# Moving one exponential behind a MoE evacuation in three units of an attention and MoE kernel

## The chip, the cores and the metric

The kernel runs on one core of one Trainium2 chip. The metric is the device time of one execution in microseconds (us). The time before is the median of three runs, 418.59 us (417.38 to 419.21). The profile is that of one further execution, which took 418.34 us.

The core's engines are called as in the profile: PE (TensorE, with PEld for its weight loads), ACT (ScalarE), DVE (VectorE), POOL (GpSimd) and SP (SyncE, which issues most DMAs). Each engine works through its own queue in order and waits on semaphores for the others.

## The reference

Attention with normalized queries and keys (8 batches, 12 heads, 448 positions, head size 64), followed by a two-layer MLP ("MoE") on 3584 tokens (768 to 2048 to 768):

```python
q_n, k_n = (rmsnorm(q, g_q), rmsnorm(k, g_k))
scores = scale * np.matmul(q_n, k_n.transpose(0, 1, 3, 2))
scores = scores - np.max(scores, axis=-1, keepdims=True)
attn = np.exp(scores)
attn = attn / (np.sum(attn, axis=-1, keepdims=True) + 1e-09)
x = np.matmul(attn, v)          # then heads side by side: (3584, 768)
h = x @ w_in
g = np.maximum(0.01 * h, h)
out = g @ w_out
```

## The kernel before

**Units and stages.** The attention is cut into 24 units, each one batch and four of its heads (three units make a batch). A unit has seven score tiles (t = 0 to 6), each of two PSUM banks. For u from 3 to 23 a unit runs through four stages, d = 0 to 3. In units 7 to 21 the scores (`score`, matmuls of line 222) of tile 0 are made in d = 0, of tiles 1, 2, 3 in d = 1, of 4, 5, 6 in d = 3 (`TRIPLES`). ACT turns each tile into exponentials (`ex`, line 242, tile `et`). `ex(u, 2)` issues the first two of a group of three straight behind the scores; the third is left in `st[u]["sT"]` and is issued later, in the unit's job list.

**MoE work between the stages.** The MLP of a batch already finished is kept in a list, `queue`, of small items. `fill(u, d, jobs)` takes as many items from it as the string `PLAN` says for this unit and stage (three in unit 8, d = 1; two in units 14 and 20, d = 1), and after each item it issues one entry of `jobs`: the remaining attention work of the stage. An item of the first layer (`moe1`) is six matmuls (line 420) into one PSUM bank and the evacuation of that bank by ACT with the leaky ReLU (`prelu`, line 414, into `gt`). Work that an item leaves for later (`later`) is issued when the next item begins (`flush`).

**The second layer** is done, for pairs of token tiles, with seven block products in place of eight (`seven`, items i0 to i6, matmuls of line 516), which need four sums of `gt` blocks made by DVE in the tile `sa`: s1 (line 497), s2 (line 500, which reads what s1 wrote), s3 (line 503) and s4 (line 506). For the first pair of an odd batch each sum is made in two halves of 128x512. i0 multiplies `gt` itself; i1 needs s2, i3 s1, i4 s3 and i5 s4. The second halves of s1 and s2 follow the last `moe1` item, whose evacuation they read; those of s3 and s4 follow i0.

**Where this meets.** In units 8, 14 and 20, d = 1, the two items taken first are the last two `moe1` items of batches 1, 3 and 5; behind them comes i0 and then i1. The jobs of that stage are the scaling of a transposed tile (`prep_g`, line 176), and the sums of squares (`prep_ssq`, line 180) with the sum of the first three exponential tiles (`add_e`, line 320, tiles 0 to 2). POOL's part in the stage is `xmul_pool` (line 376), the multiplication of the previous unit's output with the reciprocal softmax sums `rz`, which SP spreads by four DMAs (line 366). Further on in DVE's queue stand the copy of the first product (line 538), additions of products (line 523), the norms of unit u+2 (`prep_norm`, line 192, which need `rinv`, lines 185 and 186 on ACT; a transposing DMA, line 209, follows them) and, in the next unit, the row maximum (line 262) and its diagonal matrix `dg` (line 264), which PE takes in line 274.

PSUM has eight banks, given out by a list in the order in which they were dropped (`aux` for one, `slot` for a pair), so the order in which ACT's evacuations are written also decides which bank comes next. The order on every engine is the order of the Python text; no scheduler changes it.

Of the kernel before, what the change touches and what calls it, by code (L numbers as in the profile page):

```python
# [18 lines left out]
def kernel(  # L19
# [62 lines left out]
    def drop(tile_):  # L82
        for i in range(8):
            if tile_ is single[i]:
                assert i not in free
                free.append(i)
                return
        x = [i for i in range(4) if tile_ is double[i]][0]
        assert 2 * x not in free and 2 * x + 1 not in free
        free.extend((2 * x, 2 * x + 1))  # L90
# [134 lines left out]
    def qk(u, steps):  # L225
        st[u]["sT"] = []
        for t in steps:
            sT = slot()
            score(u, t, (sT[:, 0], sT[:, 1]))
            st[u]["sT"].append((t, sT))  # L230

    def ex(u, most=NS):
        s = st[u]
        if "et" not in s:
            s["et"] = epool.tile([P, NS, 2, S], FP16, tag="et", name="et")
        for t, sT in s["sT"][:most]:
            if isinstance(sT, list):
                for a in range(2):
                    nc.scalar.activation(s["et"][:, t, a], sT[a][:, 0:S], AF.Exp, bias=s["eb"], scale=1.0)
                    drop(sT[a])  # L240
            else:
                nc.scalar.activation(s["et"][:, t], sT[:, :, 0:S], AF.Exp, bias=s["eb"], scale=1.0)  # L242
                drop(sT)
        s["sT"] = s["sT"][most:]
# [6 lines left out]
    def shift_max(u):  # L251
        s = st[u]
        sT = s["sT"][0][1]
        if isinstance(sT, list):
            pm2 = small.tile([P, 2], FP32, tag="pm2", name="pm2")
            for a in range(2):
                nc.vector.tensor_reduce(pm2[:, a:a + 1], sT[a][:, 0:S], axis=AXL.X, op=ALU.max)
            s["spare"] = sT[0]
            nc.vector.tensor_reduce(s["spare"][:, 511:512], pm2, axis=AXL.X, op=ALU.max)
        else:  # L260
            s["spare"] = sT[:, 0]
            nc.vector.tensor_reduce(s["spare"][:, 511:512], sT[:, :, 0:S], axis=AXL.XY, op=ALU.max)  # L262
        s["dg"] = small.tile([P, P], FP16, tag="dg", name="dg")
        nc.vector.tensor_tensor(s["dg"], ident16, s["spare"][:, 511:512].broadcast_to([P, P]), op=ALU.mult)
# [22 lines left out]
    def gate(u):  # L287
        nc.gpsimd.tensor_copy(gate_t, buf(u, "n16")[:, 1, NS - 1, 1, D - 1:D])
# [38 lines left out]
    def zcol(u):  # L327
        s = st[u]
        s["zc"] = aux()
        ets = z_tiles(u)  # L330
        for i, e in enumerate(ets):
            for y in range(2):
                for a in range(2):
                    c = 32 * (2 * y + a)
                    nc.tensor.matmul(s["zc"][c:c + 32, 0:HS], onesr, e[:, a, HS * y:HS * y + HS],  # L335
                                     start=(i == 0), stop=(i == len(ets) - 1))

    def pv_slot(u):
        s = st[u]
        s["pslot"] = slot()  # L340
        s["pv"] = [s["pslot"][:, r] for r in range(2)]
        pv(u)
# [25 lines left out]
    def xmul_sb(u):  # L368
        xmul_pool(u, nc.vector)
# [76 lines left out]
    def flush(keep=0):  # L446
        kept = [p for p in pend if keep and (p[0] in (s1, s2, s3, s4) or hasattr(p[0], "waits") or keep == 5 and hasattr(p[0], "copies"))]
        now = [p for p in pend if p not in kept]
        pend[:] = kept
        for fn, args in now:  # L450
            fn(*args)
# [270 lines left out]
    def also(fn, *more):  # L722
        def both():
            fn()
            for m in more:
                m()
        return both
# [52 lines left out]
    def tripled(u):  # L780
        return 7 <= u < NU - 2

    def narrow(u):
        return 3 <= u < NU - 1
# [34 lines left out]
    with tc.manual_schedule():  # L819
# [203 lines left out]
        for u in range(3, NU):  # L1023
            for d in range(4):
                if u == 7 and d == 0:
                    shared.append(u)
                if d > 0 or u > 3:
                    qk(u, (TRIPLES if tripled(u) else STEPS)[d])
                    if d == 0:
                        shift_max(u)  # L1030
                        flush()
                        if u in (5, 6):
                            xmul_sb(u - 2)
                        if narrow(u - 1):
                            pv_slot(u - 1)
                            zcol(u - 1)
                            shift_mm(u)
                            pv_out(u - 1)
                        else:
                            zsum_slot(u - 1)  # L1040
                            pv(u - 1)
                            shift_mm(u)
                            zinv(u - 1)
                    ex(u, 2)
                    if d == 0 and narrow(u - 1):
                        zcol_ln(u - 1)
                if d == 2 and (u == 3 or ADDED.get(u, 0) > 3) and u < NU - 1:
                    add_e(u)
                    if u > 4:
                        xmul_sb(u - 1)  # L1050
                jobs = []

                def job(fn, *args):
                    jobs.append(lambda: fn(*args))

                if d == 0:
                    if u == 3:
                        prep_norm(4)
                        gate(4)
                    elif narrow(u - 1):  # L1060
                        if u < NU - 1:
                            job(zcol_inv, u - 1)
                    else:
                        xmul(u - 1)
                    if u + 4 < NU:
                        job(load, u + 4)
                    if u + 3 < NU:
                        load_v(u + 3)
                    if u < 6:
                        prep_sqp(u + 3)  # L1070
                if d == 1 and narrow(u - 1) and not 5 <= u < 8 and ADDED.get(u, 0) < 4:
                    xmul_pool(u - 1)
                if u == NU - 1:
                    if d == 1:
                        job(zcol_inv, u - 1)
                if fed(u, d) and u > 3:
                    push(u // NQ - 1)
                if (u, d) in ((3, 1), (4, 0)):
                    for ti in range(2):
                        prep_tr(u + 1, ti, VV)  # L1080
                if d == 1 and 5 <= u < NU - 1:
                    job(prep_g, u + 1)
                if u + 2 < NU:
                    if d == 1:
                        if ADDED.get(u) == 3 and u > 3:
                            job(lambda u: (prep_ssq(u + 2), add_e(u)), u)
                        else:
                            for ti in range(2):
                                job(prep_ssq, u + 2, ALL, (ti,))
                    if d == 2:  # L1090
                        job(prep_rinv, u + 2)
                        if u == 6:
                            job(xmul_sb, u - 1)
                        for ti in range(2):
                            job(prep_norm, u + 2, ALL, (ti,))
                        if u > 3:
                            job(prep_trd, u + 2)
                if d == 1 and 4 <= u < 8:
                    job(weight_sum, u - 4, 0)
                if d == 0 and 5 <= u < 9:  # L1100
                    job(weight_sum, u - 5, 1)
                if d == 1 and u == NU - 2:
                    jobs.append(lambda: None)
                    job(add_e, u)
                if u == NU - 2 and d == 0:
                    for n, tile_ in ((1, (raws, "rq", 3)), (2, (raws, "rk", 3)), (3, None), (4, (prep_p, "sq", 3))):
                        job(win_sum, n, 1, tile_)
                    for n in (3, 1, 2, 4):
                        job(x_sum, LATE, n)
                if u == NU - 1 and d == 3:  # L1110
                    job(add_e, u)
                    job(xmul_sb, u - 1)
                if d == 3 and 6 <= u < NU - 3:
                    for ti in range(2):
                        job(prep_sq, u + 3, ALL, (ti,))
                if st[u]["sT"]:
                    jobs[0:1] = [also(lambda: ex(u), *jobs[0:1])]
                fill(u, d, jobs)
        zsum_slot(NU - 1)
        pv(NU - 1)  # L1120
# [37 lines left out]
```

## Time and profile before

| | us |
|---|---|
| median of the runs (lowest to highest) | 418.59 (417.38 to 419.21) |
| the profiled execution | 418.34 |
| its span, first to last instruction | 416.6 |
| PE busy | 396.9 (95%) |
| DVE busy | 310.3 (74%) |
| ACT busy | 299.2 (72%) |
| POOL busy | 68.9 (17%) |
| mean granted clock of TensorE | 0.999 |

Busy time is what an engine's instructions cover; matmuls overlap each other, so a busy PE may still lose time between two starts. A timeline line gives the start in the span, the duration, engine, source line, operation, tile written and tiles read, shapes and count; in brackets, the idle time of that engine just before it and what ended it. A line of the list of waits gives who waited for whom, the total, the number of times and the longest.

### The profile page before, as it was taken

Reading aid. Unit: us, or ns where it says so; the run is one execution under the profiler, and the core shown is the slowest. Engines: PE = TensorE matmul, PEld = TensorE weight load, DVE = VectorE, ACT = ScalarE, POOL = GpSimd, SP = SyncE. Lnnn points to the kernel's source line nnn. Section 1 sums busy time; section 2 is a strip of 40 time slices with the busy share of each in tenths; the row PEclk is TensorE's granted clock in tenths of the full one; section 3 lists DMA queues with packets and bytes.
Section 4 is the critical chain, followed back from the end, with each engine's and each line's share of the span. In section 5 each row is a group of like instructions: output and inputs, shape, how many; then the busy total and the mean of one; then the engine's idle time right before and its main releaser. Section 6 shows DMA issues by size and latency. Waiting matters only on the chain.

```text
span 416.6 us, 9411 instructions
## 1 busy us (share of the span) xinstructions
PE 396.9 (95%) x3840; PEld 223.6 (54%) x3840; DVE 310.3 (74%) x490; ACT 299.2 (72%) x470; POOL 68.9 (17%) x70
## 2 busy tenths in 40 slices
PE   8688999999989999999989999999998999999996
PEld 7455454455445554555445554555454557558963
DVE  5997789899777766767668767678568888667772
ACT  5998977677958689878976689877994668653600
POOL 1887432200010100020020100003011201000000
PEclk9999999999999999999999999999999999999999
DMA  5999999898654895677663796577642451032014
GB/s 189 271 238 251 237 232 238 211 190 199 139 149 71 228 216 119 162 193 167 155 155 60 207 200 153 138 159 176 198 89 46 120 135 32 2 83 76 2 30 123
DMA packets 72526, 62.87 MB, mean 151 GB/s; under 512 B 36388, under 2 KB 67620, under 8 KB 72484
## 3 DMA queue, kind: packets, MB, share of 16 engines
q1 hardware_dynamic: 61888, 50.08, 46.8%
q0 software_dynamic: 10272, 11.80, 17.9%
q8 instruction: 30, 0.49, 0.5%
q10 hardware_dynamic: 324, 0.39, 0.3%
q14 instruction: 12, 0.10, 0.1%
HBM read 45.61 MB, written 11.01 MB: 136 GB/s over the span
## 4 chain that ended last, share of the span: by engine, by line
PE 72%; ACT 10%; DVE 10%; DMA 5%; issue 2%; SPq 0%; DVEq 0%; ACTq 0%
PE banks L516 22%; PE banks L420 22%; PE banks L222 7%; PE banks L648 6%; ACT et L242 6%; PE banks L398 5%; PE banks L466 4%; DMA qkT<-n 3%; PE banks L335 2%; ACT gt L414 2%; DVE n L192 2%; DVE sa L497 2%; DVE ssq L180 1%; DMA rk<-in_k_dram 1%; DMA out_dram<-ost 1%
## 5 line engine op out<-in xcount | busy, mean ns | idle before, releaser
L242 ACT ACTIVATE et<-banks,eb 128x896 f16<-128x896 f32 x166 | 160.3, 1015 | 29.3 <-PE banks L222 16.6
L420 PE MATMUL banks<-xt,win 128*128 128x448 f16 x612 | 122.2, 353 | 0.0
L420 PEld LDWEIGHTS <-win 128*128 128x128 f16 x612 | 57.3, 98 | 55.8 <-issue 6.5
L414 ACT ACTIVATE gt<-banks 128x448 f16<-128x448 f32 x104 | 56.7, 565 | 5.8 <-PE banks L420 4.6
L222 PE MATMUL banks<-qkT 64*64 64x448 f16 x672 | 50.8, 362 | 4.3 <-ACT et L242 3.4
L516 PE MATMUL banks<-tw,sa 128*128 128x384 f16 x264 | 47.4, 326 | 6.1 <-DVE sa L500 6.1
L180 DVE TENSOR_REDUCE ssq<-sq 128x14 f32<-128x896 f32 (+2 forms) x49 | 50.2, 1058 | 1.2 <-ACT sq L169 1.2
L516 PEld LDWEIGHTS <-sa 128*128 128x128 f16 x352 | 33.1, 98 | 31.5 <-DVE sa L500 7.3
L149 POOL DMA_DIRECT2D vt<-in_v_dram x24 | 17.9, 746 | 169.8 <-PE banks L398 169.5
L523 DVE TENSOR_TENSOR ost<-banks,ost 128x384 f32<-128x384 f32 x55 | 30.4, 553 | 17.2 <-PE banks L516 16.0
L398 PE MATMUL banks<-et,vt 64*64 64x448 f16 x672 | 37.0, 349 | 0.1
L222 PEld LDWEIGHTS <-qkT 64*64 64x64 f16 x672 | 17.9, 104 | 35.4 <-issue 28.4
L516 PEld LDWEIGHTS <-gt 128*128 128x128 f16 x264 | 25.5, 98 | 18.0 <-issue 1.4
L262 DVE TENSOR_REDUCE banks<-banks 128x1 f32<-128x896 f32 x22 | 24.1, 1096 | 14.7 <-PE banks L222 10.9
L466 PE MATMUL banks<-wout,gt 128*128 128x384 f16 x192 | 34.1, 327 | 0.0
L376 POOL TENSOR_TENSOR xt<-x,rz 128x896 f16<-128x896 f32 x9 | 19.4, 2159 | 81.8 <-DMA rz<-zs 74.3
L516 PE MATMUL banks<-wout,gt 128*128 128x384 f16 x176 | 32.4, 326 | 0.0
L192 DVE TENSOR_TENSOR n<-rq,rinv 128x896 f16<-128x896 f32 (+2 forms) x25 | 27.3, 1095 | 2.9 <-ACT rinv L186 2.9
L350 ACT COPY x<-banks 128x896 f32<-128x896 f32 x16 | 14.5, 906 | 20.6 <-DVE banks L275 20.6
L192 DVE TENSOR_TENSOR n<-rk,rinv 128x896 f16<-128x896 f32 (+2 forms) x26 | 27.5, 1065 | 0.0
L549 ACT COPY ost<-banks 128x384 f32<-128x384 f32 x11 | 5.3, 478 | 29.8 <-PE banks L516 29.7
L398 PEld LDWEIGHTS <-vt 64*64 64x64 f16 x672 | 20.3, 107 | 10.6 <-issue 0.4
(103 smaller groups left out, 482.9 us busy)
## 6 DMA issues: line engine op xcount, KB each, us to landing
rq<-in_q_dram SPq DMA_DIRECT2D x24, 448.0 KB, 4.3
rk<-in_k_dram SPq DMA_DIRECT2D x24, 448.0 KB, 4.7
out_dram<-ost SPq DMA_DIRECT2D x52, 192.0 KB, 3.5
rz<-zs SPq DMA_DIRECT2D x80, 112.0 KB, 2.3
vt<-in_v_dram POOLq DMA_DIRECT2D x24, 224.0 KB, 5.5
win<-in_moe_w_in_dram POOLq DMA_DIRECT2D x8, 384.0 KB, 15.8
wout<-in_moe_w_out_dram POOLq DMA_DIRECT2D x2, 1536.0 KB, 28.2
out_dram<-ost SPq DMA_DIRECT2D x4, 96.0 KB, 2.1
```

The lines of the kernel that those rows point to most:

```text
L180: nc.vector.tensor_reduce(buf(u, "ssq")[:, ti, :, c[0]:c[1]], buf(u, f"sq{ti}")[:, :, c[0]:c[1]], axis=AXL.X, op=ALU.add)
L192: nc.vector.tensor_tensor(buf(u, "n16")[:, ti, c[0]:c[1]].rearrange("p s a d -> p a s d"), src[:, :, c[0]:c[1]], buf(u, "rinv")[:, ti, :, ...
L222: nc.tensor.matmul(banks[a][64 * r:64 * r + 64, 0:S].rearrange("p (t x) -> p t x", t=NS), kT(u, r, a, t), qT(u, r, a), start=True, stop=True)
L242: nc.scalar.activation(s["et"][:, t], sT[:, :, 0:S], AF.Exp, bias=s["eb"], scale=1.0)
L262: nc.vector.tensor_reduce(s["spare"][:, 511:512], sT[:, :, 0:S], axis=AXL.XY, op=ALU.max)
L398: nc.tensor.matmul(s["pv"][r][64 * a:64 * a + 64, 0:S], vts[u % NV][64 * r:64 * r + 64, a, t], s["et"][64 * r:64 * r + 64, t, a], start=(t ...
L414: nc.scalar.activation(dst, src, AF.Prelu, bias=0.0, scale=1.0, alpha=0.01)
L420: nc.tensor.matmul(hps[:, 0:S], win16[:, kt // 2, kt % 2, ts(ft, P)], xt[:, kt // 2, kt % 2], start=(kt == 0), stop=(kt == KT - 1))
L466: nc.tensor.matmul(op2[:, 0:HC], gt[:, ft, ds(col(t), P)], wout16[:, ft, ds(HC * half, HC)], start=(i == 0), stop=(i == FT - 1))
L516: nc.tensor.matmul(bank[:, 0:HC], a[:, f], b[:, f], start=(first and f == 0), stop=(f == HF - 1), skip_group_check=not first)
L523: nc.vector.tensor_tensor(dst, g[name][:, 0:HC], src, op=ALU.add)
L648: nc.tensor.matmul(bank[:, HX * i:HX * i + HX].rearrange("p (t x) -> p t x", t=NS), w, x[:, kt], start=start, stop=(kt == HK - 1), skip_gr ...
```

## The change

```diff
                 if st[u]["sT"]:
-                    jobs[0:1] = [also(lambda: ex(u), *jobs[0:1])]
+                    n = 1 if d == 1 and u % 6 == 2 else 0
+                    jobs[n:n + 1] = [also(lambda: ex(u), *jobs[n:n + 1])]
                 fill(u, d, jobs)
```

The remaining exponential of a group is put in front of the first job, that is, behind the first MoE item. In units 8, 14 and 20 (u % 6 == 2, d = 1) it is now put in front of the second job, behind the second item. On ACT the order "evacuation, exponential of tile 3, evacuation" becomes "evacuation, evacuation, exponential of tile 3". The order on PE, DVE, POOL and SP stays as it was. Because the exponential's two banks are dropped after the second evacuation's bank, the PSUM pairs 4/5 and 6/7 take each other's place in what follows, from each of the three units on.

## The prediction

> **What bounds the kernel now.** I read the page's busy shares first, then the list of who waited for whom on TensorE, then the timeline around the longest wait, engine by engine. The page says that PE is the engine to follow:
>
> ```profile
> PE 396.9 (95%) x3840; PEld 223.6 (54%) x3840; DVE 310.3 (74%) x490; ACT 299.2 (72%) x470; POOL 68.9 (17%) x70
> ```
>
> The waits of PE (columns: total us, times, longest us) name one wait that is larger than all others:
>
> ```profile
> PE banks L516 <- DVE sa L500: 6.1, 3, 2.1
> PE banks L222 <- ACT et L242: 3.4, 8, 0.7
> ```
>
> Line 500 is s2, one of the four sums that feed the seven products. Its three waits lie at 123.0, 218.8 and 314.5 us, in units 8, 14 and 20: the units that the change touches. From 97 us to the end PE has no other gap over 0.08 us, so what is gained here has nothing else to hide behind. Unit 14 in the timeline (start, duration, engine, line; in brackets the idle time and what ended it):
>
> ```profile
> 214.01 0.60 ACT L414 ACTIVATE gt<-banks 128x448 f16<-128x448 f32 x1
> ...
> 214.44 1.07 ACT L242 ACTIVATE et<-banks,eb 128x896 f16<-128x896 f32 x1
> 214.60 1.46 PE L516 MATMUL banks<-wout,gt 128*128 128x384 f16 x8
> ...
> 215.32 0.62 ACT L414 ACTIVATE gt<-banks 128x448 f16<-128x448 f32 x1
> ...
> 215.89 2.06 POOL L376 TENSOR_TENSOR xt<-x,rz 128x896 f16<-128x896 f32 x1 [7.25 <-DMA rz<-zs]
> 215.90 0.81 PE L516 MATMUL banks<-tw,sa 128*128 128x384 f16 x4
> 215.97 2.26 DVE L497 TENSOR_TENSOR sa<-gt 128x512 f16<-128x512 f16 x1 [1.14 <-ACT gt L414]
> ...
> 218.27 0.42 DVE L500 TENSOR_TENSOR sa<-sa,gt 128x512 f16<-128x512 f16 x1
> 218.61 0.55 DVE L538 COPY ost<-banks 128x384 f32<-128x384 f32 x1
> 218.75 0.44 PEld L516 LDWEIGHTS <-sa 128*128 128x128 f16 x4 [2.43 <-DVE sa L500]
> 218.75 0.82 PE L516 MATMUL banks<-tw,sa 128*128 128x384 f16 x4 [2.04 <-DVE sa L500]
> 219.08 0.41 DVE L503 TENSOR_TENSOR sa<-gt 128x512 f16<-128x512 f16 x1
> ```
>
> The chain is: third exponential (214.44), second evacuation (215.32 to 215.94), s1 on line 497 (215.97), s2 (218.27), PE (218.75). What is long in it is s1: 2.26 us. Eleven microseconds earlier the other half of the same sums, the same shape, took this:
>
> ```profile
> 203.72 0.42 DVE L497 TENSOR_TENSOR sa<-gt 128x512 f16<-128x512 f16 x1
> 204.17 0.42 DVE L500 TENSOR_TENSOR sa<-sa,gt 128x512 f16<-128x512 f16 x1
> ```
>
> The difference is the multiplication on POOL (line 376), which starts 0.08 us ahead of s1 and ends at 217.95; s1 ends 0.28 later. So DVE stood still for POOL's whole instruction. That it works the other way round too, a third place shows:
>
> ```profile
> 280.98 1.09 DVE L192 TENSOR_TENSOR n<-rq,rinv 128x896 f16<-128x896 f32 x1
> 281.15 2.86 POOL L376 TENSOR_TENSOR xt<-x,rz 128x896 f16<-128x896 f32 x1 [7.93 <-DMA rz<-zs]
> ...
> 282.45 2.51 DVE L192 TENSOR_TENSOR n<-rk,rinv 128x896 f16<-128x896 f32 x1
> ```
>
> Here DVE began 0.17 us before POOL and kept its 1.09 us; POOL took 2.86 instead of its usual 2.06; and the next norm, begun inside POOL's time, took 2.51 instead of 1.08. Whoever starts first runs through. DVE instructions that read PSUM (the 0.55 us copies and additions) run at their usual length beside POOL.
>
> **The change, part by part.** Per unit one exponential (1.07 us shown, 0.90 from start to start) changes places with one evacuation on ACT. Nothing is added or removed; PE, DVE, POOL and SP keep their order, and no DMA is issued by the moved step or passed by it.
>
> *The evacuation comes earlier.* Now it starts at 215.32 because the exponential holds ACT. Without it, ACT is free at 214.44, but the matmuls of the second item must be done: their group ends at 214.76 by the PE timeline. Where an evacuation waits for such a group (ten times on this page), it starts 0.04 us after that end and takes 0.54: one at 100.71 follows a group that ends at 100.67. So it runs from 214.80 to 215.34 instead of ending at 215.94: 0.60 us earlier. ACT now waits 0.19 us for PE, a new wait. Behind it stand the exponential, then lines 185 and 186 (rinv).
>
> *s1 and s2.* s1 starts 0.03 us after the evacuation ends, as now: 215.37. DVE is free then (last addition of line 320 ended at 214.84). s1 takes 0.42 and ends at 215.79, and s2 starts 0.035 us behind it (0.03 to 0.04 in all pairs of this shape): 215.82. POOL starts at 215.89. It waits for the rz transfers, which hang on nothing that moves. So s2 starts 0.07 us ahead of POOL, runs 0.42, and is done at 216.25. In unit 8 the same sum gives 120.065 against POOL at 120.15 (0.085 ahead), in unit 20 311.57 against 311.64 (0.065 ahead).
>
> *Whether 0.07 us is enough* is the disputed size. Bounds from the rows: POOL ahead by 0.07 wins (215.89 against 215.97), DVE ahead by 0.17 wins (281.15). In between no row stands. In the blocked pairs, s1's 0.42 leaves 0.28 after POOL's end, so at most 0.14 passes between DVE's start and its claim; POOL's loss of 0.80 us against the 0.92 that DVE still had to run leaves 0.12 for POOL's own start and DVE's release together. The point of balance then lies between DVE 0.14 ahead and POOL 0.12 ahead. I take the middle, equal starts, so s2 wins; both ends stay in the range. POOL's start also depends on transfers: from the issue of the first rz transfer to POOL's start it is 4.36, 4.35 and 4.35 us in the three units, and 4.33 to 4.79 in five others. The scatter is mostly towards later, which helps.
>
> On this the Trainium skill, "SBUF — State Buffer", section "Who interferes with whom", agrees that a VectorE instruction with two SBUF inputs and a GpSimd instruction that reads SBUF exclude each other for a whole instruction, the first to issue winning; by that rule all three stalls go. Against it speaks "Perfetto Trace Analysis", section "GPSIMD Engine Instruction": a GpSimd span in a profile is to be taken as unreliable, so a lead of 0.07 us read from it may be none; by that the gain would be only that of the first rival below. The three units' agreement within 0.02 us speaks for the first.
>
> *PE.* With s2 done at 216.25 and 0.06 us for the signal (218.69 to 218.75 now), PE may go on at 216.31. Its four matmuls from 215.90, at 0.1625 us each from start to start (eight in 1.30), end their turn at 216.55. So PE doesn't wait at all, and what follows starts at 216.55 instead of 218.75: 2.20 us, more than the 2.04 shown as idle, because a matmul's record is longer than its turn. Unit 8: 120.14 + 0.65 = 120.79 instead of 123.01, 2.22. Unit 20: 2.20. **Sum 6.63 us.**
>
> *What is late next.* The exponential now ends at about 216.3 instead of 215.5. Only the scores of tiles 4 to 6 want its PSUM slot, which PE reaches at 218.6: covered by 2.3 us; each microsecond beyond would be a microsecond of PE. The PSUM pairs 4/5 and 6/7 change roles afterwards, with no other wait added on any engine. rinv is ready at about 216.9, and the norm wants it at 218.8.
> POOL's instruction now runs from about 216.2 to 218.3, on s3 and s4 (lines 503, 506) instead of s1. s3 would start at 216.63, ends at about 218.5, s4 at 218.9; PE wants s3 in the fifth product at 222.8 - 2.2 = 220.6, covered by 2 us. Then the two norms and an addition fall 1.25 us behind PE's new time; the addition at 223.01 has waited 0.72 for PE, which takes the lag to 0.46, the next one to 0.23. With that the row maximum (line 262, 224.79) and dg (226.20) are late; PE wants dg at 226.44, which leaves 0.19 after the signal. PE loses about 0.05 us. The transposing DMA that follows the norms comes 1.0 us earlier than now, lands in 4.2 (at most 6.4), and DVE wants its result at 227.9: covered by 0.1 to 2.3. For all this I take 0.05 us a unit, bounds 0 to 0.2.
>
> **Sum.** 6.63 - 0.15 = 6.5 us. The profiled execution took 418.34 us (span 416.6 and 1.7 around it): 411.8. The median of the runs lies 0.25 above it, so I forecast **412.0 us**.
>
> **The rivals.**
> 1. *POOL claims before s2.* For: 0.07 us is less than the 0.14 bound, and s1 and s2 are two instructions with 0.03 us between them. Then s2 is held to POOL's end: 217.95 + 0.28 + 0.06 = 218.29 instead of 218.75, 0.46 us a unit, 1.4 in all: 417.0. Chance 0.11.
> 2. *Units differ.* The leads differ by 0.02 us and transfers scatter. One unit lost gives 413.8, two 415.5. Chance 0.09.
> 3. *Nothing moves.* If the evacuation were held by something other than the exponential, or PE's next group waited for another half of the sums, the time stays at 418.6. Against it: the chain of waits runs through exactly these five pieces. Chance 0.03.
> 4. *Slower: TensorE's clock.* The pauses are the only rests PE has after 97 us. If without them the granted clock fell from 123 us on, each per cent would cost 2.9 us of the 294 left; the gain is gone below 0.978, and 0.97 would give some 421. Against it: the 93 us between two pauses ran at 1.00 with PE full. Chance 0.03.
>
> **How the numbers follow.** The forecast gets 0.74. The range takes its own scatter (runs of before spread from 417.4 to 419.2, so 1.2 below) and rival 2: 410.8 to 415.5, which leaves out rivals 1, 3 and 4 (0.17). Faster by over 0.5% (2.1 us, about what a measurement of this kernel can tell from no change) are the forecast and rival 2: 0.83. Rivals 1 and 3 lie within 0.5%: 0.14. Slower: 0.03.
>
> **What the profile after would show.** The wait of PE for line 500 gone from its list; line 497 at 0.42 us in all eight short instances; in each of the three units s2 ahead of POOL, POOL's 2.06 grown to about 2.4, and line 503 grown to about 1.9. If line 500 takes about 2.4 us behind a 0.42 us line 497, rival 1 has it. I am wrong if those rows are as I say and PE is late elsewhere, above all at line 274 (dg) or line 222.

## The result, and the profile after

The changed kernel took 412.98 us (median of 4 runs, 412.51 to 413.63) beside 418.88 us before in the same comparison: a ratio of 0.9867 (95% interval 0.9838 to 0.9896). A second comparison gave 413.23 beside 418.82, ratio 0.9868 (0.9843 to 0.9893). The profiled execution took 412.78 us. One run further down, the second of the fourth experiment (426.1 us at a mean clock of 0.948), was disturbed and is left out.

The first page lines of the kernel after:

```profile
span 411.0 us, 9411 instructions
...
PE 395.8 (96%) x3840; PEld 223.8 (54%) x3840; DVE 308.7 (75%) x490; ACT 299.6 (73%) x470; POOL 69.3 (17%) x70
```

PE's waits after (columns: total us, times, longest us): line 500 is gone from the list, and a line stands there that was not in it before.

```profile
PE banks L222 <- ACT et L242: 3.4, 8, 0.7
PE banks L516 <- DVE ost L523: 2.0, 2, 1.0
```

Unit 14 in the timeline of the kernel after:

```profile
211.38 1.46 PE L516 MATMUL banks<-wout,gt 128*128 128x384 f16 x8
...
211.59 0.54 ACT L414 ACTIVATE gt<-banks 128x448 f16<-128x448 f32 x1 [0.18 <-PE banks L420]
212.03 1.00 ACT L242 ACTIVATE et<-banks,eb 128x896 f16<-128x896 f32 x1
212.16 0.43 DVE L497 TENSOR_TENSOR sa<-gt 128x512 f16<-128x512 f16 x1 [0.54 <-ACT gt L414]
...
212.62 0.42 DVE L500 TENSOR_TENSOR sa<-sa,gt 128x512 f16<-128x512 f16 x1
212.68 2.30 POOL L376 TENSOR_TENSOR xt<-x,rz 128x896 f16<-128x896 f32 x1 [7.26 <-DMA rz<-zs]
212.69 1.46 PE L516 MATMUL banks<-tw,sa 128*128 128x384 f16 x8
...
213.43 1.83 DVE L503 TENSOR_TENSOR sa<-gt 128x512 f16<-128x512 f16 x1
...
215.19 0.41 DVE L506 TENSOR_TENSOR sa<-gt,sa 128x512 f16<-128x512 f16 x1
...
215.53 1.08 DVE L192 TENSOR_TENSOR n<-rq,rinv 128x896 f16<-128x896 f32 x1
...
216.53 0.54 DVE L523 TENSOR_TENSOR ost<-banks,ost 128x384 f32<-128x384 f32 x1
217.00 1.07 DVE L192 TENSOR_TENSOR n<-rk,rinv 128x896 f16<-128x896 f32 x1
217.12 1.14 PE L516 MATMUL banks<-tw,sa 128*128 128x384 f16 x6 [0.98 <-DVE ost L523]
```

The reader sees the forecast chain in the first half. The evacuation takes 0.54 us straight behind its matmuls, s1 and s2 take 0.43 and 0.42, s2 starts 0.06 us ahead of POOL, and the eight matmuls of the second product run in one piece at 212.69. POOL's instruction has grown to 2.30, and s3 (line 503) to 1.83. The second half shows a wait that was not forecast: at 217.12 the fourth product (i3) starts 0.98 us late, held by the addition of line 523, which stands in DVE's queue behind the first norm (line 192). In the kernel before, the same two instructions stood so:

```profile
220.75 0.55 DVE L523 TENSOR_TENSOR ost<-banks,ost 128x384 f32<-128x384 f32 x1
221.50 2.77 PE L516 MATMUL banks<-tw,sa 128*128 128x384 f16 x16
```

There the addition ended at 221.30, 0.20 us ahead of the product, so nobody waited for it.

In unit 8 the order on DVE is another, and no wait follows (DVE alone, kernel after):

```profile
121.62 0.41 DVE L506 TENSOR_TENSOR sa<-gt,sa 128x512 f16<-128x512 f16 x1
121.95 0.55 DVE L523 TENSOR_TENSOR ost<-banks,ost 128x384 f32<-128x384 f32 x1
122.42 1.08 DVE L192 TENSOR_TENSOR n<-rq,rinv 128x896 f16<-128x896 f32 x1
```

**Where the time went, by PE's starts.** Matmul by matmul the two traces can be laid side by side, since PE's order is the same. At 97 us (before) the kernel after is already 1.05 us ahead, though the programs don't differ up to there: start-up scatter (the sixth experiment's kernel, without the change, is 1.05 us ahead there too). Over the three pauses it gains 2.20, 2.21 and 2.21; behind units 14 and 20 it gives back 1.04 each. That is 1.05 + 6.62 - 2.08 = 5.6 us, the difference of the profiled executions (418.34 - 412.78). The change itself accounts for 4.5 of it. The medians differ by 5.6 to 5.9; the eighth and ninth experiment deal with that remainder.

### The profile page after: what moved, and what is told of

Read it like the earlier page. It is cut to its first block, busy times and chain, and to the rows that moved or that the text cites. A ratio compares the mean times of both kernels' runs of the same rounds, so it can differ in the third digit from the quotient of the medians.

```text
span 411.0 us, 9411 instructions
## 1 busy us (share of the span) xinstructions
PE 395.8 (96%) x3840; PEld 223.8 (54%) x3840; DVE 308.7 (75%) x490; ACT 299.6 (73%) x470; POOL 69.3 (17%) x70
## 4 chain that ended last, share of the span: by engine, by line
PE 86%; DVE 6%; ACT 5%; issue 1%; DMA 1%; DVEq 0%; ACTq 0%
PE banks L420 28%; PE banks L516 22%; PE banks L222 9%; PE banks L466 8%; PE banks L398 7%; PE banks L648 6%; ACT et L242 3%; PE banks L335 3%; PE banks L817 2%; DVE n L192 1%; DMA out_dram<-ost 1%; PE banks L274 1%; PE banks L204 1%; DVE xt L407 1%; ACT et L239 1%
## 5 line engine op out<-in xcount | busy, mean ns | idle before, releaser
L222 PEld LDWEIGHTS <-qkT 64*64 64x64 f16 x672 | 17.8, 104 | 35.4 <-issue 28.6
L516 PEld LDWEIGHTS <-gt 128*128 128x128 f16 x264 | 25.5, 98 | 18.0 <-issue 1.4
L466 PEld LDWEIGHTS <-gt 128*128 128x128 f16 x192 | 17.7, 98 | 13.8 <-issue 3.2
```

The costliest lines, as they stand in the source:

```text
L222: nc.tensor.matmul(banks[a][64 * r:64 * r + 64, 0:S].rearrange("p (t x) -> p t x", t=NS), kT(u, r, a, t), qT(u, r, a), start=True, stop=True)
L466: nc.tensor.matmul(op2[:, 0:HC], gt[:, ft, ds(col(t), P)], wout16[:, ft, ds(HC * half, HC)], start=(i == 0), stop=(i == FT - 1))
L516: nc.tensor.matmul(bank[:, 0:HC], a[:, f], b[:, f], start=(first and f == 0), stop=(f == HF - 1), skip_group_check=not first)
```

## The experiments

**The changed kernel again** (no edit).

> The changed kernel once more, for its size. The two profiles side by side say: each of the three pauses gone (2.20 us each from start to start, 6.6 together), two new pauses of 1.0 us on TensorE in units 14 and 20 (waiting for an addition on line 523), and 1.05 us that differ before 100 us, where both programs are the same. Theory A (port): the change is worth 6.6 - 2.0 = 4.5 us, ratio 0.989, and the rest of the first measurement (5.9 us) is start-up scatter. Rival: the start-up difference belongs to the change, then 5.6 us, ratio 0.9866.

Measured: 413.23 beside 418.82, ratio 0.9868 (0.9843 to 0.9893). The profile repeats the steps: 2.21, 2.20 and 2.22 gained, 1.05 given back in units 14 and 20. So the steps are the change's, but theory A's total of 0.989 is not confirmed: 0.9868 lies at the rival's figure, although the interval reaches to 0.9893. The rival's reason does not hold either, for in this profile the kernel is only 0.33 us ahead at 97 us. Something else distinguishes the runs. The profile also has a wait of 0.46 us in unit 9: the rz transfers came 1.5 us later there (POOL's idle time 8.60 instead of 7.12), so that POOL's multiplication met a norm, 2.77 us instead of 1.30.

**The norms one item later in units 14 and 20.**

```diff
                         if u == 6:
                             job(xmul_sb, u - 1)
+                        if u in (14, 20):
+                            jobs.append(lambda: None)
                         for ti in range(2):
                             job(prep_norm, u + 2, ALL, (ti,))
```

> The changed kernel with the two norms of units 14 and 20 issued one MoE item later, so that the addition of the second product stands ahead of them in VectorE's queue, as it does in unit 8. Theory A: the new pauses are the addition, which frees the PSUM bank that the third product takes, queued behind a norm of 1.08 us; they go, 2.0 us less than the changed kernel in the same job. Rival B: the third product is late because of the moved exponential or the exchanged PSUM pairs; then the two pauses of 1.0 us stay and the time is that of the changed kernel.

Measured: 410.83 beside 413.23 for the changed kernel in the same job, 2.4 us less (2.0 by PE's starts, as expected), and 0.981 (0.9785 to 0.9834) of the kernel before. Unit 14 on DVE in this kernel:

```profile
213.88 1.84 DVE L503 TENSOR_TENSOR sa<-gt 128x512 f16<-128x512 f16 x1
215.64 0.41 DVE L506 TENSOR_TENSOR sa<-gt,sa 128x512 f16<-128x512 f16 x1
215.98 0.54 DVE L523 TENSOR_TENSOR ost<-banks,ost 128x384 f32<-128x384 f32 x1
216.44 1.07 DVE L192 TENSOR_TENSOR n<-rq,rinv 128x896 f16<-128x896 f32 x1
```

The addition comes directly behind s4, and no wait of PE for line 523 is left. The moved exponential and the exchanged PSUM pairs are as in the changed kernel, so rival B falls. The wait is one for a PSUM bank. By the kernel's list of banks the third product (i2) adds onto the first product's bank, and the fourth (i3) takes the bank of the second, which this addition empties. (The expectations of this experiment and of the sixth call the fourth product the third.)

**The kernel before without POOL's multiplication in units 8, 14 and 20.**

```diff
                 if d == 1 and narrow(u - 1) and not 5 <= u < 8 and ADDED.get(u, 0) < 4:
-                    xmul_pool(u - 1)
+                    if u not in (8, 14, 20):
+                        xmul_pool(u - 1)
...
                         job(prep_rinv, u + 2)
+                        if u in (8, 14, 20):
+                            xcopy_act(u - 1)    # nc.scalar.copy(xts[b][:, g], st[u]["x32"])
```

> The kernel before, with POOL's multiplication left out in units 8, 14 and 20: a plain copy on ScalarE, in a stretch where it is idle, takes its place, so three units of attention output are not divided by their softmax sums. ScalarE's order is that of before up to the second evacuation. Theory A: s1 falls from 2.26 to 0.42 us in these units, TensorE resumes at about 216.9 instead of 218.75, and of each pause of 2.20 some 0.36 stay: 1.84 x 3 = 5.5 us less than before, some 413. Rival C, by which the gain is the evacuation coming 0.6 us earlier and POOL's overlap an accident: no change, 418.6.

Measured: 412.29, ratio 0.9848 (0.9816 to 0.988). The lines of this kernel are numbered six higher. Unit 14 on DVE, s1 and s2:

```profile
213.38 0.43 DVE L503 TENSOR_TENSOR sa<-gt 128x512 f16<-128x512 f16 x1 [1.14 <-ACT gt L420]
213.84 0.43 DVE L506 TENSOR_TENSOR sa<-sa,gt 128x512 f16<-128x512 f16 x1
```

and what is left of PE's wait for s2:

```profile
PE banks L522 <- DVE sa L506: 0.6, 3, 0.2
```

The evacuation comes as late as before (DVE still idles 1.14 us for it), and yet s1 takes 0.43 and PE gains 1.83 us in each unit by its starts, 1.84 forecast. So POOL's instruction was the cause of the pauses; the order on ACT matters only because it decides on which side of POOL's start s1 and s2 fall. Rival C falls.

**s2 delayed by a little.**

```diff
+    DELAY = {1: 92, 3: 132, 5: 180}
...
+                more = [lambda f=f, x=x: later(f, tt, half[x]) for f in fs]
+                if n == FT - 1 and b in DELAY and not late:
+                    more.insert(1, lambda: later(pause, DELAY[b]))   # nc.vector.tensor_reduce of DELAY[b] elements
```

> The changed kernel with a small VectorE reduction between s1 and s2, of 92, 132 and 180 elements in units 8, 14 and 20. By the lengths of such reductions in the trace (0.16 us and about 1 ns per element) s2 starts 0.06, 0.10 and 0.15 us later. It led POOL by 0.08, 0.06 and 0.035, so it should start 0.02 ahead of POOL in unit 8, 0.04 behind in unit 14 and 0.11 behind in unit 20. Theory A: behind POOL s2 takes about 2.3 us and TensorE's pause is back at some 1.7 us from start to start (POOL's start + 2.06 + 0.34 against the turn's end), surely in unit 20; where the balance lies, units 8 and 14 show. Rival C: a delay of 0.15 us is covered by TensorE's margin of 0.25, no pause anywhere.

Measured: 414.21 us in its profiled run, the only one used, so the rows count here and not the time. Units 8 and 14 of this kernel:

```profile
118.73 0.42 DVE L500 TENSOR_TENSOR sa<-sa,gt 128x512 f16<-128x512 f16 x1
118.75 1.46 PE L516 MATMUL banks<-tw,sa 128*128 128x384 f16 x8
118.79 2.30 POOL L376 TENSOR_TENSOR xt<-x,rz 128x896 f16<-128x896 f32 x1 [7.29 <-DMA rz<-zs]
```

```profile
212.35 2.06 POOL L376 TENSOR_TENSOR xt<-x,rz 128x896 f16<-128x896 f32 x1 [7.25 <-DMA rz<-zs]
212.36 0.81 PE L516 MATMUL banks<-tw,sa 128*128 128x384 f16 x4
212.38 2.32 DVE L500 TENSOR_TENSOR sa<-sa,gt 128x512 f16<-128x512 f16 x1
```

In unit 8 the reduction delayed s2 by less than expected; it still led POOL by 0.06 us and ran in 0.42. In unit 14 it started 0.03 us behind and took 2.32; in unit 20 0.06 behind, 2.28. PE's starts gained only 0.46 and 0.45 us there, against 2.2 in unit 8: the pauses are back, and rival C falls. In the changed kernel itself unit 20 won with a lead of 0.035 us, and in the profile of the sixth experiment s1 of unit 8 started 0.014 us behind POOL and took 2.33. So the balance lies between 0.035 us ahead and 0.014 us behind, and a tenth of a microsecond is worth 1.8.

On this the Trainium skill ("SBUF — State Buffer", section "Who interferes with whom": the first to issue has the shared ports for the whole instruction) agrees with the rows; the warning of "Perfetto Trace Analysis", section "GPSIMD Engine Instruction", that GpSimd spans are unreliable, did not show here: the recorded order of the starts decided in every case of the eleven profiles, and each s1, s2 or s3 that was held ended 0.28 to 0.29 us after POOL's recorded end.

**The changed kernel without POOL's multiplication in those units** (the same edit as above, on the changed kernel).

> The changed kernel with POOL's multiplication left out in units 8, 14 and 20 (a plain copy on ScalarE in its place: three units of attention output are not divided by their softmax sums). Theory A, second half: the new pauses of units 14 and 20 begin with s3 (1.83 us instead of 0.42) held by POOL, which puts the norm and the addition behind it late; without POOL s3 is back at 0.42 and both pauses go although the norm still stands ahead of the addition: 2.0 us less than the changed kernel, some 411. Rival B (order in VectorE's queue alone, POOL has no part): pauses of 1.0 us stay, some 413.

Measured: 411.03, ratio to before 0.9798 (0.9754 to 0.9841). s3, s4 and what follows in unit 14, lines again six higher:

```profile
214.30 0.41 DVE L509 TENSOR_TENSOR sa<-gt 128x512 f16<-128x512 f16 x1
214.63 0.42 DVE L512 TENSOR_TENSOR sa<-gt,sa 128x512 f16<-128x512 f16 x1
215.23 1.09 DVE L192 TENSOR_TENSOR n<-rq,rinv 128x896 f16<-128x896 f32 x1 [0.18 <-ACT rinv L186]
216.24 0.55 DVE L529 TENSOR_TENSOR ost<-banks,ost 128x384 f32<-128x384 f32 x1
```

The norm stands ahead of the addition as in the changed kernel, but DVE reaches it with time to spare, and PE has no wait here. So the new wait needs both: POOL holding s3 for 1.4 us, and the norm ahead of the addition. Taking away either one removes it.

**The norms later, without the change.**

> The kernel before with the norms of units 14 and 20 issued one item later, without the change. Theory A: before, the addition ended 0.2 us ahead of the third product's turn, so its place in the queue was covered; the three pauses of 2.2 us stay: no change, 418.6 within 0.5. Rival D: the norms' place is worth its 2 us by itself and the second experiment shows two separate gains: some 416.6.

Measured: 418.97 beside 419.33, ratio 0.9991 (0.9963 to 1.0019), and the three pauses at s2 are in its profile (6.2 us). The norms' place is worth nothing before the change: rival D falls. This profile showed something else. Its stretches around unit 8 (columns: stretch, length, busy us of PE, PEld, DVE, ACT, POOL with counts; then the granted clock of PE, the DMA share and GB/s):

```profile
118.00:121.00 3.00, 1.91 (x12) 0.94 (x10) 1.86 (x2) 1.58 (x4) 1.83 (x1) 1.00 0.92 278
121.00:124.00 3.00, 1.97 (x7) 0.97 (x8) 2.73 (x7) 0.00 (x0) 0.24 (x1) 0.71 0.18 68
124.00:127.00 3.00, 3.00 (x22) 1.22 (x21) 1.91 (x2) 1.12 (x2) 0.00 (x0) 0.72 0.00 0
127.00:130.00 3.00, 3.00 (x34) 1.68 (x36) 1.88 (x4) 3.00 (x5) 0.00 (x0) 1.00 0.82 153
```

The pause ended at 122.03. Right behind it the clock fell, 0.29 and 0.28 of 3 us each: 1.7 us of clock, which is 3.4 us at one half. Matmuls that otherwise start every 0.1625 us started every 0.32, and by PE's starts 1.7 us were lost.

**The change in unit 8 alone.**

```diff
-                    n = 1 if d == 1 and u % 6 == 2 else 0
+                    n = 1 if d == 1 and u == 8 else 0
```

> The change in unit 8 alone. Theory A: the units add up, and unit 8, where the addition already stands ahead of the norms, has no new pause: one pause of 2.2 us less, ratio 0.9947, while units 14 and 20 keep their pauses at s2 of 2.2 us. Rival E: what unit 8 gains is given back later, with the exchanged PSUM pairs: a ratio near 1.

Measured: 416.27 beside 419.33, ratio 0.9931 (0.9901 to 0.9961), which holds the 0.9947 expected. By PE's starts 2.21 us are gained in unit 8 and nothing is given back, so rival E falls. In this profile the half clock came behind the pause of unit 14 that was left (0.71 and 0.72 in the stretches from 217 to 223 us) and took 1.6 us by PE's starts.

**Longer pauses.** The fourth experiment's edit on the kernel before, with 768 elements in each of the three units.

> The kernel before with a VectorE reduction of 768 elements between s1 and s2 in units 8, 14 and 20, which makes each of the three pauses about 0.8 us longer (3.0 instead of 2.2 from start to start). Theory F: a pause is dearer than its length, because behind some of them TensorE is granted half its clock for 3.41 us (1.7 us lost), as in the profiles of the sixth and seventh experiment, and the longer the pause the oftener; then the time is over 2.4 us above before, some 2.4 to 6, the mean clock of the runs lies below that of before, and the profile shows 0.5 behind at least one pause. Rival G: the half clock has nothing to do with the pauses: 2.4 us more, mean clocks as before.

Measured: 423.5 beside 419.47, ratio 1.0101 (1.0068 to 1.0134), 4.0 us more; mean clocks of its runs 0.986 to 0.994, those of before in this job 0.991 to 0.999. Its pauses and the stretches around unit 8:

```profile
PE banks L516 <- DVE sa L500: 8.4, 3, 2.8
```

```profile
121.00:124.00 3.00, 0.94 (x5) 0.57 (x6) 3.00 (x6) 0.00 (x0) 0.53 (x1) 0.93 0.29 110
124.00:127.00 3.00, 3.00 (x17) 1.19 (x18) 2.64 (x4) 0.36 (x1) 0.00 (x0) 0.50 0.02 5
127.00:130.00 3.00, 3.00 (x28) 1.56 (x20) 1.05 (x2) 2.94 (x5) 0.00 (x0) 1.00 0.78 144
```

Two of its three pauses, those of units 8 and 20, are followed by half clock. Rival G falls: 0.8 us more pause three times cost 4.0 by the medians, not 2.4. By PE's starts the longer pauses cost 2.2 us in this profile and the two pieces of half clock 1.6 each; 0.3 went to a wait at line 274 near 362 us that no run explains.

The clock records also show when a pause is followed by half clock. In the profiles of experiments six to eight each such piece fills one step of a fixed grid of 3.41 us (the full clock between two pieces lasts a whole number of steps, such as 194.56 us or 57 of them). The steps ahead of the four pieces that came behind pauses held 1.29 us of PE's work (sixth experiment, 118.85 to 122.26 us), 1.34 (seventh) and 0.62 and 0.64 (eighth): the whole pause lay inside the step. Where a step's end cut the pause in two, both steps held 1.38 us or more, and no half clock followed, before (1.87, 2.06 and 2.23 in the emptier step) as in the eighth experiment's unit 14 (1.38). So by these profiles it is the place of the pause on the grid, which lies differently in each of them, that makes it dear. The amount of work alone does not settle it: in the first 32 us steps with 1.5 us of work and more were followed by half clock too, and so was one with 1.40 behind the last matmuls of the changed kernel.

**The norms later, on the changed kernel, again.**

> The second experiment's kernel once more, as the version without any pause on TensorE from 97 us to the end. Theory F: mean clocks of 0.995 to 1.0 in all runs, no half clock after 100 us, 410.8 within 0.5, ratio to before 0.980 to 0.983, more than the 6.5 us (0.9845) that its three pauses are long. Rival G: mean clocks spread as before's, 0.991 among them, and a ratio near 0.9845.

Measured: 410.84 beside 419.47, ratio 0.9788 (0.9746 to 0.9831); mean clocks 0.996 to 1.0 in six runs. As expected by F, it gains more than the 6.5 us that the pauses of before were long, and rival G's 0.9845 lies outside the interval; F's range of 0.980 to 0.983 was a little too high. Its profile has no half clock after 100 us; its one piece lies at 28.6 to 32.0 us, in the start-up. This is the fastest version here: 2.4 us below the changed kernel in the second experiment's job.

## Why the prediction was right, and where it was not

The range (410.8 to 415.5) held 412.98, the forecast 412.0 was 1.0 us low, and the direction was right. Step by step:

- *What bounds the kernel* was right: the three pauses, and POOL's instruction as their cause (third experiment, which left ACT's late evacuation in place).
- *The evacuation earlier*: right to 0.01 us: 0.18 us of waiting, 0.54 of duration.
- *s1, s2 and POOL*: forecast leads 0.085, 0.07 and 0.065; measured 0.08, 0.06 and 0.035. The disputed point, taken as equal starts between bounds of 0.14 and 0.12, lies within 0.035 of that. It was close: had unit 20's lead been 0.05 us shorter, s2 would have started 0.014 behind POOL, where the sixth experiment's s1 lost, and rival 2 would have come. POOL grew to 2.29 to 2.33 us (about 2.4 forecast), s3 to 1.83 (about 1.9).
- *PE*: 2.20 to 2.22 forecast per unit, 2.20 to 2.21 measured, 6.6 us in all. The gain is larger than the idle time that the list of waits shows, as reckoned.
- *What is late next* is the step that failed. I followed DVE's lag of about 1.25 us to the row maximum and dg and took 0.05 us a unit, bounds 0 to 0.2. The addition of line 523 was in that lag, but I asked only when it got its input, not who waited for its output: it empties the PSUM bank that the fourth product takes. The profile of before had the size already: the addition was 0.20 us ahead of that product, so a lag of 1.25 makes PE 1.05 late. Measured 1.04 us in units 14 and 20, nothing in unit 8, where the addition stands ahead of the norms: 2.1 us in place of 0.15. The prediction allowed for PE being late elsewhere, but looked for it at lines 274 and 222, not at line 516.
- *The clock* (rival 4) had the wrong sign. I took the pauses for rests whose loss might lower the clock. The profiles of experiments six to eight show the opposite: a pause of 2.2 us is in some executions followed by 3.4 us at half clock, 1.6 to 1.7 us lost. In the eleven runs of before in the second comparison the mean clock was 0.991 to 0.995 in seven; in the eleven of the version without pauses (second and ninth experiment) it was never under 0.996. Of runs with 0.998 or more, before's median is 417.2 (4 runs) and the changed kernel's 412.6 (4 runs, same job): 4.6 us, which is what PE's starts give. The other microsecond of the medians thus goes with the clock. That it comes from the half clock behind pauses in just those runs is inferred from their mean clocks; only profiled runs show where in the run the clock fell, and no run of before with a low clock was profiled. Start-up has a part too: five of the eleven profiles have one or two pieces of half clock in the first 32 us, before any of the three pauses.

So the forecast owed its nearness in part to two errors of opposite sign, 2 us of new waiting and about 1 us of clock.

The Trainium skill, "TensorE: Matmul & The Clock Gate", section "What's actually happening", describes a free-running activity window of about 3.4 us after which the clock is halved or restored. The 3.4 us of half clock here fit it. Its section "HAM oscillation — how this bites in real kernels" gives idle gaps over about 3.4 us as the harmful ones; here 2.1 us of idle time was enough where it fell inside one step of the grid, and the measurement decides.

## What to carry to other kernels

When a stall is removed, list for every instruction that now runs relatively later not only what it needs but what it frees: a late addition that empties a PSUM bank stalls the matmul that takes the bank as surely as a late input. An instruction on VectorE that takes five times its usual length beside a GpSimd instruction points to the two excluding each other; a swap elsewhere that moves it across the other's start by a tenth of a microsecond can be worth more than the operation's own length. And a pause of TensorE may cost more than it lasts, so compare runs by their granted clock as well as by their time.

## What the runs showed of the hardware

- VectorE additions with both inputs in SBUF and GpSimd's multiplication exclude each other for a whole instruction: 2.24 to 2.33 us for s1 or s2 behind POOL, 0.42 ahead of it; POOL grew from 2.06 to between 2.27 and 2.33 when it came second to s2. VectorE instructions on PSUM (0.55 us) ran beside it unchanged.
- The start order in the trace decided, down to 0.035 us ahead and 0.014 us behind.
- After 100 us TensorE's half clock came in pieces of 3.4 us on a fixed grid, right behind pauses of 2.1 us (one of three, and one of two, in two profiles; none of three in that of before) and of 2.8 us (two of three), never behind the pauses of 1.6 us in the fourth experiment or the waits of 1.0 us in two profiles. The four pauses that were followed by one lay inside a single step of the grid; those that a step's end cut in two were not followed by any.
